# Leaky ReLU as one activation, and the second batch's k, numerators and kv in two parts each

## The chip, the core and the metric

The kernel runs on one core of a Trainium2 chip. The time is device time in microseconds (us) of one execution. Engines are named as in the profile: PE (TensorE matmul), PEld (its weight load), DVE (VectorE), ACT (ScalarE), POOL (GpSimd) and SP (SyncE, which here only issues DMAs).

## The reference

Three stages follow one another: linear attention with a feature map, a first MLP with leaky ReLU, and a second one of four experts. Cut to what is computed (batch 4, heads 8, sequence 576, head 64, 128 features):

```python
def phi(x):
    proj = einsum('bhsd,df->bhsf', x, w_phi)
    proj = proj - max(abs(proj), axis=-1, keepdims=True)
    return concatenate([exp(proj), exp(-proj)], axis=-1)
q_p, k_p = phi(q), phi(k)
kv  = einsum('bhsf,bhsd->bhfd', k_p, v)
z   = sum(k_p, axis=2)
num = einsum('bhsf,bhfd->bhsd', q_p, kv)
den = einsum('bhsf,bhf->bhs', q_p, z)[..., None] + 1e-06
x   = (num / den)                 # as 2304 tokens x 512
h   = x @ w_in                    # 512 x 2048
x   = maximum(0.01 * h, h) @ w_out    # 2048 x 512
# for each expert e of 4, p = domain_probs normalized:
out += p[:, e] * (maximum(x @ w1[e], 0) @ w2[e])
```

## The kernel before

Everything is in one program with four batches. For each batch the attention is done by head pairs (four per batch), and its output x stays on chip as xh and xl, one part of 128 rows for each head pair. The first MLP of a batch is done in 16 blocks of 128 hidden rows, in groups of four. The second MLP comes after the last batch's first MLP, from about 640 us, and the change doesn't touch it.

**Precision.** A matmul of plain f32 operands is recorded as two passes. In the other way an operand is written as a high part in fp32r and a low part (operand less high part, also fp32r), and three matmuls are made: high by high, high by low, low by high. The helper `hilo` (line 113) makes the parts: the high one as a copy on ACT (L117) or as a cast on DVE (L115; `VHI`, line 67, says which names go to DVE), the low one always as a subtraction on DVE (L118). `DIRECT` (line 37) says for each batch which operands stay plain f32: k (`k_prep`, L172, and the projection L204), n (the numerators with their e and kv: `kv_side` L250, `q_exp` L310, `q_num` L335) and q (the queries). Where kv is in two parts they are kvh and kvl (L258, L259); where k is, they are kh and kl; where e is, qh and ql.

**The attention's steps.** `load`, `load_v`, `load_q` bring kraw, v and qraw. `k_feat` makes in three parts the projection pk (PE L204), its absolute maximum m (DVE L209), the difference ky (DVE L216) and the exponentials kp and kt (ACT L227). `kv_side` accumulates kvp (PE L242). `q_prep` makes qr: a cast (DVE L273, or ACT L275) and its low part (DVE L276). `q_proj` makes pq (PE L292), copies it to pc (ACT) and reduces it over partitions to mb on POOL (L296). `q_sub` subtracts (DVE L301), `q_exp` makes e (ACT), and `q_num` the numerators nm (PE L335), which ACT copies to nf. `x_den` and `x_rec` bring the denominators ds by DMA into a small tile, make their reciprocals, write them to a scratch dr in DRAM (L362) and read them back spread over partitions as rb (L365). `x_mul` multiplies to xr (DVE L381) and splits it to xh (ACT) and xl (DVE L118).

**The first MLP.** `moe1_up` makes hp in PSUM (PE L506, 24 matmuls of 288 columns for each block), from it hs, 0.01 times it (ACT L518), and g, the larger of both (DVE L520), and splits g to gt. `moe1_down` (PE L538) accumulates op over four blocks. In batch 0 the weights come as 64-bit words: `w64_dma` (L445) loads 1 MB as r64, `w64_split` converts on ACT (L460) and DVE (L461, L464, L467) to w32, splits that to wt (L117, L118), and stores w32 to DRAM (L471), where the later batches load it.

**Order.** The steps of an attention have due times (`TIMES`), by which they are sorted; those of batch b+1 are spread over the first MLP of batch b (`LO`, `HI`). A scheduler with a simulated timeline then orders the instructions of each engine. Each engine works strictly in its order, and SP's one queue issues nearly all loads and stores. SBUF tiles of one row of 576 come from one pool of 19 buffers, whatever their name; PSUM tiles come from a pool of three buffers (hp, op, pq, the wide pk) and one of two (pk, kvp, nm).

Of the kernel before, what the change touches and what calls it, by code (L numbers as in the profile page):

```python
# [10 lines left out]
AF = mybir.ActivationFunctionType  # L11
ALU = mybir.AluOpType
# [21 lines left out]
WIDE = (1, 0, 0, 0)  # L34
INPL = (1, 0, 1, 0)

DIRECT = ('knq', 'kn', '', '')

TIMES = (
    (  # L40
# [39 lines left out]
def body(ctx, tc, kT, qT, vh, w_phi, w_in, w_out, probs, w1, w2, out):  # L80
    nc = tc.nc
# [22 lines left out]
    def unit(name, dt=F32):  # L104
        return up.tile([128, S], dt, tag="u", name=name)

    def two(name):
        return ps2.tile([128, 2, 512], F32, tag="two", name=name)
# [4 lines left out]
    def hilo(hi, lo, src, name, b):  # L113
        if name in VHI[min(b, 2)]:
            nc.vector.tensor_copy(hi, src)  # L115
        else:
            nc.scalar.copy(out=hi, in_=src)  # L117
        nc.vector.tensor_tensor(out=lo, in0=src, in1=hi.bitcast(F32), op=ALU.subtract)  # L118
# [52 lines left out]
    def k_prep(b, hp):  # L171
        kraw = raws[b, hp]  # L172
        if "k" in DIRECT[b]:
            kfs[b, hp] = kraw, None
# [56 lines left out]
    def kv_side(b, hp, h):  # L231
# [17 lines left out]
        if h == 1:  # L249
            if "n" in DIRECT[b]:  # L250
                kv = up.tile([128, 4, 128], F32, tag="u", name="kv")
# [14 lines left out]
    def q_prep(b, h):  # L266
        qraw = raws[b, "q", h]
        if "q" in DIRECT[b]:
            qrs[b, h] = qraw
# [11 lines left out]
    def q_proj(b, h):  # L281
        qr = qrs.pop((b, h))
        pq = two("pq")
        for n in range(2):
            o = pq[:, n, 0:HS]
            xs_ = qr[:, n * HS : (n + 1) * HS]
            if "q" in DIRECT[b]:

# [17 lines left out]
    def q_exp(b, h, n):  # L306
        mb = ys[b, h]
        e = unit("e")
        for j in range(2):
# [5 lines left out]
            )  # L315
        if "n" in DIRECT[b]:
            es[b, h, n] = e, None
# [100 lines left out]
    def attn(b, lo, hi):  # L418

        A = []  # L420
        for p in range(NP):
            T = TIMES[p if b == 0 else NP]
            for t, (f, h, a) in zip(T, STEPS):
                i = p if h is None else 2 * p + h
                A.append((p + t, lambda f=f, i=i, a=a: f(b, i, *a)))
        A.sort(key=lambda x: x[0])
        t0, t1 = A[0][0], A[-1][0]
        return [(lo + (hi - lo) * (t - t0) / (t1 - t0), f) for t, f in A]
# [68 lines left out]
    def moe1_up(F, n):  # L497
        x = xs[F // NF]
        wi = wt1[0, F]
        if n == 0:  # L500
            hps[F] = two("hp")
        hp = hps[F]
        for kk in range(KK):
            assert ("x", F // NF, kk) in made
            for i, (a, z) in enumerate(PASS):
                nc.tensor.matmul(  # L506
                    hp[:, n, 0:HS],
                    lhsT=wi[:, a, kk * 128 : (kk + 1) * 128],
                    rhs=x[z][:, kk, n * HS : (n + 1) * HS],
                    start=(kk == 0 and i == 0),  # L510
                    stop=(kk == KK - 1 and i == 2),
                )
        if n == 0:
            return
        hv = hp[:, :, 0:HS]
        hs = unit("hs")
        hs3 = hs.rearrange("p (a s) -> p a s", a=2)
        nc.scalar.mul(out=hs3, in_=hv, mul=0.01)  # L518
        g = unit("g")
        nc.vector.tensor_tensor(  # L520
            out=g.rearrange("p (a s) -> p a s", a=2), in0=hv, in1=hs3, op=ALU.max
        )
        gt = gp.tile([128, 2, S], F32R, tag="g", name="gt")
        hilo(gt[:, 0], gt[:, 1], g, 'g', F // NF + 1)
        gts[F] = gt
# [27 lines left out]
    def moe1_group(G):  # L553


        def up(F, n):
            if n == 0:
                w1_dma(0, F + 2)
                w1_split(0, F + 1)
                w1_dma(1, F)  # L560
            elif F:
                w1_split(1, F - 1)
            moe1_up(F, n)

        def down(d, n):
            if G == B * NF // GF and d == 0 and n == 0:
                w1_split(1, G * GF - 1)
            moe1_down(G - 1, d, n)

        M = []  # L570
        for kind, i in ORDER:
            if kind == "u" and G < B * NF // GF:
                M += [lambda i=i, n=n: up(G * GF + i, n) for n in range(2)]
            elif kind == "d" and G > 0:
                M += [lambda i=i, n=n: down(i, n) for n in range(2)]
        return M
# [96 lines left out]
    def w2_sums(r):  # L673
        pool, tag = (m2["r"], "r") if m2 else (wp, "w")
        s = pool.tile([128, 4, 256], F32, tag=tag, name="rs")
        for o, x, y, op in (
            (s[:, 0], r[:, 0], r[:, 1], ALU.add),
            (s[:, 1], s[:, 0], r[:, 2], ALU.subtract),
            (s[:, 2], r[:, 2], r[:, 0], ALU.subtract),
            (s[:, 3], r[:, 3], s[:, 1], ALU.subtract),  # L680
        ):
            kept(nc.gpsimd.tensor_tensor(out=o, in0=x, in1=y, op=op))  # L682
        return s
# [158 lines left out]
    def spread(fs, lo, hi):  # L842
        return [(lo + (hi - lo) * i / len(fs), f) for i, f in enumerate(fs)]
# [9 lines left out]
    for b in range(B):  # L853
# [3 lines left out]
        if b + 1 < B:  # L857
            a = attn(b + 1, b + LO[b], b + HI[b])
        else:
            early = x2_steps(0)  # L860
            a = spread(early[:4], b + 0.1, b + 0.9)
# [11 lines left out]
    s = w2_sums(r)  # L873
# [64 lines left out]
```

## Time and profile before

| what | us |
|---|---|
| three runs | 1379.39, 1382.25, 1383.28 |
| their median | 1382.25 |
| the profiled execution | 1380.63 |
| its span | 1378.8 |

The span of the profiled execution is 1.8 us shorter than its time. Over the span PE is busy 98%, PEld 92%, DVE 59%, ACT 48% and POOL 41%. These shares are averages over stages: up to about 110 us batch 0's attention is alone, or overlaps with the first blocks of its MLP; from there to about 610 us run the first MLPs of all batches with the attention of the next ones; then comes the second MLP. A wait is read from the timeline, where the idle time ahead of an instruction stands in brackets with what ended it. A busy PE may run at a low granted clock, or with gaps between short matmuls, so its spacing is read too.

### The profile page before, as it was taken

Reading aid. Unit: us, or ns where it says so; the run is one execution under the profiler, and the core shown is the slowest. Engines: PE = TensorE matmul, PEld = TensorE weight load, DVE = VectorE, ACT = ScalarE, POOL = GpSimd, SP = SyncE. Lnnn points to the kernel's source line nnn. Section 1 sums busy time; section 2 is a strip of 40 time slices with the busy share of each in tenths; the row PEclk is TensorE's granted clock in tenths of the full one; section 3 lists DMA queues with packets and bytes.
Section 4 is the critical chain, followed back from the end, with each engine's and each line's share of the span. In section 5 each row is a group of like instructions: output and inputs, shape, how many; then the busy total and the mean of one; then the engine's idle time right before and its main releaser. Section 6 shows DMA issues by size and latency. Waiting matters only on the chain.

```text
span 1378.8 us, 21301 instructions
## 1 busy us (share of the span) xinstructions
PE 1352.1 (98%) x8105; PEld 1262.2 (92%) x8105; DVE 817.8 (59%) x1285; ACT 657.9 (48%) x1201; POOL 567.8 (41%) x398
## 2 busy tenths in 40 slices
PE   8979999999999999999999999999999999999998
PEld 6778999999999999998999999999999999899997
DVE  4589999678786656553555445445454444554444
ACT  5657657676576435424343443434443343433331
POOL 3211102111111000027767666767767675565651
PEclk9989999999999999999999999999999999999999
DMA  6466645333332222302212122321121232122111
GB/s 220 113 217 234 220 167 166 111 120 105 109 103 66 75 86 73 104 24 94 75 61 77 62 68 71 107 77 62 62 77 62 77 107 77 62 64 76 61 62 62
DMA packets 78518, 134.94 MB, mean 98 GB/s; under 512 B 12240, under 2 KB 22608, under 8 KB 78416
## 3 DMA queue, kind: packets, MB, share of 16 engines
q1 hardware_dynamic: 78416, 133.58, 29.8%
q8 instruction: 64, 1.05, 0.3%
q14 instruction: 38, 0.31, 0.1%
HBM read 120.30 MB, written 13.18 MB: 97 GB/s over the span
## 4 chain that ended last, share of the span: by engine, by line
PE 95%; DVE 1%; DMA 1%; issue 1%; ACT 1%; POOL 1%; SPq 0%; POOLq 0%; ACTq 0%; DVEq 0%
PE po L761 29%; PE hp L506 15%; PE op L538 14%; PE py L722 11%; PE pv L722 7%; PE px L722 7%; PE kvp L242 5%; PE nm L335 4%; PE pk L204 2%; PE pq L292 1%; PE pq L289 1%; DMA qraw<-qT 1%; POOL wul L704 0%; DMA r<-w 0%; DMA ds<-nf 0%
## 5 line engine op out<-in xcount | busy, mean ns | idle before, releaser
L761 PE MATMUL po<-wd,gh 128*128 128x512 f32 x1152 | 387.7, 391 | 0.9 <-POOL wd L714 0.9
L777 DVE SCALAR_TENSOR_TENSOR ob<-po,pe,ob 128x512 f32<-128x512 f32 x270 | 201.6, 749 | 216.6 <-PE po L761 216.6
L761 PEld LDWEIGHTS po<-wd,gh 128*128 128x128 f32 x1152 | 216.6, 188 | 42.3 <-POOL wd L714 1.3
L761 PE MATMUL po<-wd,gl 128*128 128x512 f32 x576 | 226.2, 393 | 0.0
L538 PE MATMUL op<-gt,wt 128*128 128x288 f32 x1536 | 219.9, 297 | 1.5 <-DVE gt L118 0.8
L296 POOL PARTITION_ALL_REDUCE mb<-pc x32 | 72.3, 2266 | 355.7 <-ACT pc L294 294.7
L506 PE MATMUL hp<-xh,wt 128*128 128x288 f32 x1024 | 216.2, 298 | 0.0
L538 PEld LDWEIGHTS op<-gt,wt 128*128 128x128 f32 x1536 | 207.9, 188 | 2.9 <-DVE gt L118 1.0
L506 PEld LDWEIGHTS hp<-xh,wt 128*128 128x128 f32 x1024 | 167.5, 188 | 1.0 <-ACT wt L117 0.3
L506 PE MATMUL hp<-xl,wt 128*128 128x288 f32 x512 | 151.8, 297 | 0.0
L714 POOL TENSOR_TENSOR wd<-r,wd 128x1024 fp32r<-128x1024 f32 x48 | 114.9, 2394 | 89.4 <-ACT wd L710 89.4
L722 PE MATMUL py<-xo,wuh 128*128 128x384 f32 x576 | 148.3, 339 | 0.7 <-DVE pz L827 0.7
L682 POOL TENSOR_TENSOR rs<-r 128x256 f32<-128x256 f32 x96 | 71.1, 741 | 188.8 <-DMA r<-w 188.8
L704 POOL TENSOR_TENSOR wul<-rs,wuh 128x1024 fp32r<-128x1024 f32 x48 | 115.5, 2406 | 65.9 <-ACT wuh L699 65.9
L704 POOL TENSOR_TENSOR wul<-r,wuh 128x768 fp32r<-128x768 f32 x48 | 88.8, 1851 | 85.7 <-ACT wuh L699 85.7
L761 PEld LDWEIGHTS po<-wd,gl 128*128 128x128 f32 x576 | 108.2, 188 | 15.2
L722 PEld LDWEIGHTS py<-xo,wuh 128*128 128x128 f32 x576 | 104.9, 188 | 4.6 <-DVE pz L827 1.0
L722 PE MATMUL px<-xo,wuh 128*128 128x384 f32 x384 | 98.9, 338 | 0.7 <-DVE acc L551 0.7
L722 PE MATMUL pv<-xo,wuh 128*128 128x384 f32 x384 | 99.1, 339 | 0.0
L722 PE MATMUL py<-xo,wul 128*128 128x384 f32 x288 | 97.3, 338 | 0.0
L506 PEld LDWEIGHTS hp<-xl,wt 128*128 128x128 f32 x512 | 96.3, 188 | 0.4
L807 ACT COPY py<-px 128x384 f32<-128x384 f32 x48 | 22.2, 463 | 143.4 <-PE px L722 137.3
(114 smaller groups left out, 2349.9 us busy)
## 6 DMA issues: line engine op xcount, KB each, us to landing
r<-w SPq DMA_DIRECT2D x192, 256.0 KB, 2.8
wr<-w SPq DMA_DIRECT2D x96, 256.0 KB, 2.7
qraw<-qT SPq DMA_DIRECT2D x32, 288.0 KB, 3.7
r<-w_out SPq DMA_DIRECT2D x9, 1024.0 KB, 9.0
r<-w_in SPq DMA_DIRECT2D x8, 1024.0 KB, 6.2
w<-w SPq DMA_DIRECT2D x32, 256.0 KB, 2.8
v<-vh SPq DMA_DIRECT2D x16, 480.0 KB, 4.0
kraw<-kT SPq DMA_DIRECT2D x16, 288.0 KB, 4.0
```

Of the source, the lines that this page charges most:

```text
L204: nc.tensor.matmul(o, lhsT=x[:, cs], rhs=w, start=(i == 0), stop=(i == len(P) - 1))
L242: nc.tensor.matmul(kvp[:, a * 128 : (a + 1) * 128], lhsT=lhs, rhs=v[:, c, h * D : h * D + 128], start=(c == 0), stop=(c == 4),)
L296: nc.gpsimd.partition_all_reduce(mb, pc, 128, bass_isa.ReduceOp.absmax)
L335: nc.tensor.matmul(o, lhsT=a[:, 2 * (h % 2) + j], rhs=x[:, j * HS : (j + 1) * HS], start=(j == 0 and i == 0), stop=(j == 1 and i == len(P) ...
L506: nc.tensor.matmul(hp[:, n, 0:HS], lhsT=wi[:, a, kk * 128 : (kk + 1) * 128], rhs=x[z][:, kk, n * HS : (n + 1) * HS], start=(kk == 0 and i ...
L538: nc.tensor.matmul(op[:, n, 0:HS], lhsT=wt1[1, C * GF + f][:, a, d * 128 : (d + 1) * 128], rhs=gts[C * GF + f][:, z, n * HS : (n + 1) * HS ...
L682: kept(nc.gpsimd.tensor_tensor(out=o, in0=x, in1=y, op=op))
L704: kept(nc.gpsimd.tensor_tensor(out=lo[:, at], in0=(r[:, 1:4], s)[i], in1=hi[:, at].bitcast(F32), op=ALU.subtract))
L714: kept(nc.gpsimd.tensor_tensor(out=d[:, 1], in0=r2, in1=d[:, 0].bitcast(F32), op=ALU.subtract))
L722: kept(nc.tensor.matmul(out, lhsT=ws[w][:, AOPS[a], kk * 128 : (kk + 1) * 128], rhs=xo[z][:, kk], start=first and n == 0, stop=n == 5, ski ...
L761: kept(nc.tensor.matmul(op, lhsT=(gh, gl)[z][:, 2 * f + t, q : q + 128], rhs=d[:, w, f], start=n == 0, stop=n == 5,))
L777: kept(nc.vector.scalar_tensor_tensor(out=o, in0=op, scalar=ps, in1=o, op0=ALU.mult, op1=ALU.add))
```

## The change

`DIRECT` loses "k" and "n" for batch 1, so its k, e and kv are written in two parts, as those of batches 2 and 3 are, and its projections and numerators are three matmuls in the place of one in plain f32. The leaky ReLU of all 64 blocks is one activation with slope 0.01 from PSUM on ACT in the place of a multiplication on ACT and a maximum on DVE. The names hs and its buffer go. The scheduler orders anew; lines from 518 on stand 3 lower.

```diff
-DIRECT = ('knq', 'kn', '', '')
+DIRECT = ('knq', '', '', '')
...
         hv = hp[:, :, 0:HS]
-        hs = unit("hs")
-        hs3 = hs.rearrange("p (a s) -> p a s", a=2)
-        nc.scalar.mul(out=hs3, in_=hv, mul=0.01)
         g = unit("g")
-        nc.vector.tensor_tensor(
-            out=g.rearrange("p (a s) -> p a s", a=2), in0=hv, in1=hs3, op=ALU.max
+        nc.scalar.activation(
+            out=g.rearrange("p (a s) -> p a s", a=2), in_=hv, func=AF.Prelu, alpha=0.01
         )
         gt = gp.tile([128, 2, S], F32R, tag="g", name="gt")
         hilo(gt[:, 0], gt[:, 1], g, 'g', F // NF + 1)
```

The first place is SP's queue around the last head pair of batch 0. In the rows, dr and rb are the reciprocals on their way to DRAM and back, r64 the 1 MB weight loads, w32 the store of a converted weight. Before:

```order
L154 DMA kraw_591<-kT 128x576
L362 DMA dr_598<-ds_564 128x9
L445 DMA r64_619<-w_in 128x2x1024
L445 DMA r64_631<-w_out 128x2x1024
L365 DMA rb_600<-dr_598 64x576 x2
L471 DMA w32_0_2_680<-w32_675 128x512
L166 DMA qraw_654<-qT 128x576
```

The same queue after:

```order
L154 DMA kraw_599<-kT 128x576
L445 DMA r64_631<-w_in 128x2x1024
L445 DMA r64_643<-w_out 128x2x1024
L362 DMA dr_606<-ds_568 128x9
L471 DMA w32_0_2_696<-w32_691 128x512
L365 DMA rb_608<-dr_606 64x576 x2
L166 DMA qraw_668<-qT 128x576
```

The write to dr moved behind both weight loads, and the store of a weight ahead of rb.

The second place is DVE's queue up to the low part of the queries of batch 1, head 5 (qr, L276). Weight steps are L461, L464, L467 and wt. Its last rows before:

```order
L467 SCALAR_TENSOR_TENSOR w32_1006<-r64_786,w32_1006 128x512
L118 TENSOR_TENSOR wt_928<-w32_921,wt_928 128x512
L461 TENSOR_SCALAR w32_1150<-w32_1150 128x512
L273 CAST qr_956<-qraw_919 128x576
L359 TENSOR_SCALAR ds_1178<-ds_1178 128x9
L118 TENSOR_TENSOR wt_979<-w32_972,wt_979 128x512
L118 TENSOR_TENSOR gt_947<-g_945,gt_947 128x576
L464 SCALAR_TENSOR_TENSOR w32_1150<-r64_970,w32_1150 128x512
L276 TENSOR_TENSOR qr_956<-qraw_919,qr_956 64x576
```

And after:

```order
L209 TENSOR_REDUCE m_1146<-pk_1139 128x4
L464 SCALAR_TENSOR_TENSOR w32_1272<-r64_1048,w32_1272 128x512
L461 TENSOR_SCALAR w32_1461<-w32_1461 128x512
L464 SCALAR_TENSOR_TENSOR w32_1429<-r64_1036,w32_1429 128x512
L118 TENSOR_TENSOR ql_1019<-e_1015,qh_1018 128x576
L273 CAST qr_1022<-qraw_975 128x576
L467 SCALAR_TENSOR_TENSOR w32_1272<-r64_1048,w32_1272 128x512
L464 SCALAR_TENSOR_TENSOR w32_1461<-r64_1048,w32_1461 128x512
L118 TENSOR_TENSOR wt_1243<-w32_1236,wt_1243 128x512
L467 SCALAR_TENSOR_TENSOR w32_1429<-r64_1036,w32_1429 128x512
L276 TENSOR_TENSOR qr_1022<-qraw_975,qr_1022 64x576
```

From the end of the last xl of batch 0 to this instruction stand 47 instructions before and 63 after; a low part ql and steps of further weights stand ahead of it now.

The third place is PE's queue where the first matmuls of the MLP begin: kvp is the kv of batch 1's first head pair, kt the last part of its k features, pk a k projection, and hp is made from batch 0's xh. Before:

```order
L292 MATMUL pq_718<-qr_593,wl_92 128x288
L242 MATMUL kvp_707<-v_446,kp_571 128x128 x4
L204 MATMUL pk_765<-wraw_89,kraw_591 128x256 x2
L242 MATMUL kvp_707<-v_446,kt_572 128x128
L242 MATMUL kvp_707<-v_446,kp_571 128x128 x4
L242 MATMUL kvp_707<-v_446,kt_572 128x128
L242 MATMUL kvp_707<-v_446,kp_571 128x128 x4
L506 MATMUL hp_633<-xh_347,wt_478 128x288
L506 MATMUL hp_685<-xh_347,wt_628 128x288
```

And after:

```order
L292 MATMUL pq_742<-qr_601,wl_92 128x288
L242 MATMUL kvp_731<-v_446,kp_575 128x128 x4
L242 MATMUL kvp_731<-v_446,kt_576 128x128
L242 MATMUL kvp_731<-v_446,kp_575 128x128 x4
L242 MATMUL kvp_731<-v_446,kt_576 128x128
L242 MATMUL kvp_731<-v_446,kp_575 128x128 x4
L242 MATMUL kvp_731<-v_446,kt_576 128x128
L242 MATMUL kvp_731<-v_446,kp_575 128x128 x2
L506 MATMUL hp_645<-xh_347,wt_478 128x288
L506 MATMUL hp_701<-xh_347,wt_640 128x288
```

The k projection of the second head pair (pk) no longer stands between the kv matmuls.

## Rows read from the trace of the kernel before

**Rows 1.** The page: busy us, share of the span and instructions of each engine.
```profile
PE 1352.1 (98%) x8105; PEld 1262.2 (92%) x8105; DVE 817.8 (59%) x1285; ACT 657.9 (48%) x1201; POOL 567.8 (41%) x398
```

**Rows 2.** Windows by stage: us, busy of PE, PEld, DVE, ACT, POOL; clock; DMA; GB/s.
```profile
0.00:110.00 110.00, 91.80 (x504) 78.69 (x505) 70.41 (x116) 64.16 (x138) 26.40 (x16) 0.91 0.58 194
110.00:600.00 490.00, 489.02 (x3712) 485.06 (x3712) 367.82 (x578) 290.10 (x561) 46.10 (x20) 1.00 0.37 118
```

**Rows 3.** Timeline of PE, 36 to 44 us: start, length, engine, line, what.
```profile
37.20 1.89 PE L204 MATMUL pk<-wraw,kraw 128*128 128x256 f32 x8
38.92 4.04 PE L335 MATMUL nm<-e,kv 128*128 128x288 f32 x16
42.80 1.05 PE L242 MATMUL kvp<-v,kp 128*128 128x128 f32 x8
```

**Rows 4.** Chain of waits, pieces of 230 to 300 and 590 to 645: start, length, what.
```profile
233.67 0.71 PE pk L204 x6
...
591.00 3.19 PE hp L506 x24
```

**Rows 5.** Window of 86 to 118 us, columns as in rows 2.
```profile
86.00:118.00 32.00, 30.10 (x209) 28.16 (x207) 29.75 (x48) 24.16 (x51) 6.46 (x3) 0.97 0.70 255
```

**Rows 6.** Groups by line, whole span, then 86 to 118: busy, mean ns, idle.
```profile
L518 ACT ACTIVATE hs<-hp 128x576 f32<-128x576 f32 x64 | 41.6, 649 | 73.5 <-PE hp L506 72.8 <-DVE mb L301 0.7
L520 DVE TENSOR_TENSOR g<-hp,hs 128x576 f32<-128x576 f32 x64 | 48.2, 753 | 45.0 <-ACT hs L518 44.9
L118 DVE TENSOR_TENSOR ql<-e,qh 128x576 fp32r<-128x576 f32 x32 | 25.1, 784 | 4.1 <-ACT qh L117 4.0
...
L467 DVE SCALAR_TENSOR_TENSOR w<-r,w 128x512 uint32<-128x512 uint32 x7 | 4.5, 680 | 0.0
L520 DVE TENSOR_TENSOR g<-hp,hs 128x576 f32<-128x576 f32 x4 | 3.0, 749 | 1.2 <-ACT hs L518 1.2
L301 DVE TENSOR_TENSOR mb<-pc,mb 128x576 f32<-128x576 f32 x2 | 2.6, 1316 | 0.0
```

**Rows 7.** Timeline of DVE; in brackets the idle time ahead and what ended it.
```profile
65.03 1.53 DVE L381 TENSOR_TENSOR xr<-nf,rb 64x576 f32<-64x576 f32 x2 [4.53 <-DMA rb<-dr]
...
80.47 0.75 DVE L381 TENSOR_TENSOR xr<-nf,rb 64x576 f32<-64x576 f32 x1 [0.82 <-DMA rb<-dr]
...
85.19 0.75 DVE L118 TENSOR_TENSOR xl<-xr,xh 128x576 fp32r<-128x576 f32 x1
...
87.05 1.89 DVE L467 SCALAR_TENSOR_TENSOR w<-r,w 128x512 uint32<-128x512 uint32 x3
...
117.20 0.76 DVE L276 TENSOR_TENSOR qr<-qraw,qr 64x576 fp32r<-64x576 f32 x1
```

**Rows 8.** Chain of waits, the piece at 118 us.
```profile
118.34 0.53 PE pq L292 x4
```

**Rows 9.** Timeline of PE: three stops.
```profile
81.66 2.05 PE L204 MATMUL pk<-wraw,kraw 128*128 128x256 f32 x4 [5.35 <-issue]
...
609.99 1.85 PE L538 MATMUL op<-gt,wt 128*128 128x288 f32 x12 [0.71 <-DVE g L520]
...
612.60 9.04 PE L538 MATMUL op<-gt,wt 128*128 128x288 f32 x66 [0.76 <-DVE gt L118]
```

**Rows 10.** Timeline of SP's queue: when it issued these DMAs.
```profile
60.89 1.10 SPq L365 DMA_DIRECT2D rb<-dr  x2
...
70.99 0.43 SPq L445 DMA_DIRECT2D r<-w_in  x1
72.73 1.10 SPq L365 DMA_DIRECT2D rb<-dr  x2
...
79.68 0.34 SPq L471 DMA_DIRECT2D w<-w  x1
```

**Rows 11.** Windows of 8 us around two stops of PE, columns as in rows 2.
```profile
58.00:66.00 8.00, 5.96 (x21) 4.32 (x19) 3.37 (x8) 3.36 (x9) 0.00 (x0) 0.79 0.39 100
74.00:82.00 8.00, 2.59 (x11) 2.16 (x10) 4.01 (x8) 4.13 (x8) 0.00 (x0) 0.51 0.83 312
```

## The prediction

> **What bounds the kernel now.** I read the page first. PE is busy 98% of the span and every other engine 59% or less [rows 1]; so the question is where PE loses time. The windows by stage tell it: PE is busy 489.02 of 490.00 us from 110 to 600, idles 18.2 us before 110 [rows 2]. A busy PE is not PE at its peak, so I looked at the spacing too: 24 matmuls on 288 columns take 3.19 us in the chain, 0.133 us each [rows 4], and none comes faster anywhere. So from 110 us on a matmul saved is time saved and a wait added is time lost; nothing later gives it back. Before 110 us the waits decide. After 640 the change touches nothing.
>
> DVE is the engine to watch. From 86 to 118 us it is busy 29.75 of 32.00 us, beside PE's 30.10 [rows 5]. One pair of rows shows how near it is: DVE ends the low part of the queries of batch 1, head 5, at 117.20 + 0.76 = 117.96 [rows 7], and PE starts the projection that needs them at 118.34 [rows 8]. I call this the anchor.
>
> **PE's own work.** An f32 matmul runs as two passes. Sixteen passes of numerators, eight matmuls, start at 38.92 and the next work at 42.80: 0.485 us each; eight passes of the k projection start at 37.20 and the next work at 38.92: 0.43 a matmul [rows 3]. In two parts a numerator is three matmuls of 0.133 = 0.40, a k chunk three of 0.118 (six in 0.71 [rows 4]) = 0.355. Batch 1 has 32 numerator matmuls and 20 k chunks: 32 x 0.086 + 20 x 0.075 = **4.3 us less** for PE, nearly all of it behind 86 us, where PE is dense.
>
> **The leaky ReLU.** It takes away 64 DVE instructions of 753 ns and puts 64 activations in the place of 64 multiplies of 649 ns [rows 6]. Prelu itself isn't in the trace; the nearest row is that multiply, an activation of the same 128x576 shape out of PSUM, and I take its 649 ns. If Prelu took twice as long, ACT would have 4 x 0.65 = 2.6 us more between 86 and 118 us, where it has 7.8 us idle [rows 5]: still no bound. By the Trainium skill (ScalarE: Activation LUTs, "What ACT_TABLE_LOAD costs") an activation with immediate operands takes 186 ns + 0.833 ns a column whatever its function, 666 ns here as an estimate; the multiply's row agrees within 3%. What DVE saves is hidden while PE is dense. It shows in one place: at the end of the first MLP the chain of multiply, maximum, high part and low part lies open, and PE waits for it twice, until 609.99 and 612.60 [rows 9]. The maximum's 0.75 us falls out of that chain: **0.75 us less**.
>
> **What the two parts cost DVE.** Batch 1 gets 4 kh, 4 kl, 16 ql (784 ns [rows 6]) and 4 kvl on DVE and 16 qh on ACT, against 16 maxima that go in batch 0's MLP. More than the total it matters where they stand. DVE works strictly in its order, so I count what stands ahead of the anchor, from the end of xl, the low part of the last x of batch 0 (85.19 + 0.75 = 85.94 [rows 7]). An instruction moves the queue on by its duration less 0.08 us (three of 0.68 [rows 6] take 1.89 [rows 7]).
> Before: 10 of 576 columns at 0.67 (gt, g, mb), 21 of 512 at 0.60 (wt, w32, ky), 2 m at 0.61, 5 shifts at 0.34, 3 qr casts at 0.41, 3 qr low parts at 0.79, three small (the kinds without a row here by their means in the view of [rows 6]): 47 instructions, 26.7 us.
> After: 14 at 0.67 (6 ql, 4 gt, 2 kl, 2 mb), 26 at 0.60, 3 at 0.61, 8 at 0.34, 3 at 0.41, 2 kh at 0.38, 3 at 0.79, four small: 63 instructions, 34.9 us. The 8.2 us more are ql, kl, kh and kvl (6.7) and the weight conversions and reductions that the order moves ahead (4.2), less four maxima (2.7).
> Before took 32.0 us for its 26.7 (85.94 to 117.96): 1.9 us of waits, and 3.4 us in which instructions were stretched, as mb to a mean of 1316 ns [rows 6], beside POOL's three reductions [rows 5]. After has three there too, so I carry the 5.3 us over. It can be 3 (a late DVE waits for less) or 9 (each ql waits for a qh that ACT makes just before).
> Here a rule speaks against the change. By the Trainium skill (SBUF — State Buffer, "Who interferes with whom") a DVE instruction with two SBUF inputs contends with GpSimd's reads, one with at most one doesn't. The maximum read PSUM and SBUF, and its mean there is 749 ns, not stretched [rows 6], as the rule has it; ql and kl read SBUF twice. By the rule one instruction is caught per reduction, and 5.3 us stay; were the loss in proportion to the queue, it would be 5.3 x 34.9 / 26.7 = 6.9, and the sum 1.6 us worse.
>
> **Up to xl.** Here SP's order decides. Before, the rb load of the last head pair was issued at 72.73, shared the DMA engines with two 1 MB loads [rows 10], and DVE got it at 80.47, 7.7 us later [rows 7]. In after it stands behind the store of a converted weight, which waits for DVE's three steps on the w_in load. But that load no longer waits for dr and starts about 3 us earlier than its 70.99; so the store, at 79.68 before, goes at some 76.7 and rb at 77.1. An rb load without such company took 4.1 us, issued at 60.89 [rows 10] and used at 65.03 [rows 7]: xr at 81.2, or 84.8 with 7.7. I take the first, since the big loads are over by then. From xr to the end of xl DVE needs 5.5 us in both orders: 86.8 against 85.94, **0.9 us later**.
> PE loses a stop of 5.35 us before 81.66 [rows 9], whose releaser the row doesn't name; by the order it is the PSUM buffer that the last ky empties, and that stands behind xr on DVE. The stop isn't won: kvp needs kt, which comes from the last ky too. PE restarts at about 82.9, with less queued, and reaches the xl matmuls at about 89 in both.
>
> **The sum.** Anchor: 86.8 + 34.9 + 5.3 = 127.0 on DVE, PE at 127.1 instead of 118.34: 8.8 us later. PE then has less left: the 4.3 saved, less 1.6 used up by then (12 k chunks, 8 numerator matmuls), plus 13 down matmuls (1.7) that the new order does earlier: 4.4. That leaves +4.4. Such a stop costs clock too: from 58 to 66 PE was busy 5.96 of 8 us and the granted clock was 0.79, which is 0.21 x 8 = 1.7 us; from 74 to 82, busy 2.59 us, it was 0.51 [rows 11]. I take **1.7**. With the end's 0.75: 4.4 + 1.7 - 0.75 = **+5.3 us**. The profiled execution's 1380.63 becomes 1385.9; by the median of the runs, 1382.25, **1387.5**.
>
> **Rivals.**
> (a) *DVE absorbs it: no change.* For it: before, DVE waited because it was early, and a late one waits for nothing. With only the 34.9 us and no clock lost the anchor is at 121.7, and 121.8 - 118.34 - 4.4 - 0.75 = -1.7 us; with the 3.4 of stretching, +1.7: 1380.5 to 1384. Against it: six qh that are made just in time.
> (b) *Only PE's saving counts: faster.* DVE does the first k parts in its idle time before xl and the projection of head 5 finds its queries ready: -4.3 - 0.75 = -5, 1377. It decides if DVE is some 9 us further at xl than I have it. Against it: the order, in which 63 instructions stand between.
> (c) *rb is late: slower still.* With 7.7 us for rb behind the store, xl and the anchor come 3.6 us later and the clock stays low as long again (1.7): +10.6, 1393. Nothing between rb's issue and xl takes it up.
> (d) The activation could ignore its slope; it would cost the same, and no time hangs on it.
>
> **How the numbers follow.** A measurement of this kernel can tell about 0.3% (4.1 us) from no change. Forecast 0.43, (a) 0.32, (c) 0.11, (b) 0.14. The forecast lies 1 us over the bound of 1386.4, so 0.06 of its 0.43 goes to the middle: slower 0.48, within 0.38, faster 0.14. The range leaves out (b) and the far half of (c): 1380 to 1394.
>
> **What would show it.** Right: in after a PE wait of 5 us or more for DVE qr L276 between 115 and 130 us, DVE without a gap ahead of it, and a low clock behind it; xl at 86 to 88; then a dense PE to 600 with numerators at 0.133 a matmul; the wait before 612 shorter by 0.75. Wrong: no such wait (a, b); rb used after 83 (c); or an activation of hp well above 0.65 us.

## The result, and the profile after

| | before | after |
|---|---|---|
| median of five runs, us | 1379.52 | 1388.70 |
| lowest and highest, us | 1377.96 to 1383.28 | 1385.69 to 1389.69 |
| profiled execution, us | 1380.63 | 1385.69 |
| its span, us | 1378.8 | 1383.6 |

The changed kernel is slower: the ratio of the runs is 1.0058, with a 95% interval of 1.0046 to 1.0069, which is 8.0 us on 1379.5 (the two medians lie 9.2 apart). The forecast was 1387.5 and "slower", with 1380 to 1394 as its range. Of the two profiled executions one is 1.1 us above its kernel's median and the other 3.0 below, so the traces show 4.8 us (the spans) of the 8.0. The 3 us between stay unexplained by them. One execution of a later run, e10, took 2235.71 us at a granted clock of 0.557 and is left out of its ratio.

The page of the changed kernel, engines over the whole span, answers to [rows 1]; PE's share fell by a point:

```profile
PE 1348.5 (97%) x8157; PEld 1264.0 (91%) x8157; DVE 797.6 (58%) x1249; ACT 664.2 (48%) x1217; POOL 569.2 (41%) x398
```

The windows of 86 to 130 us, columns as in [rows 2], tell where: of before first,

```profile
86.00:130.00 44.00, 42.10 (x290) 39.48 (x288) 41.72 (x69) 31.97 (x66) 9.62 (x4) 0.98 0.69 248
```

and of after:

```profile
86.00:130.00 44.00, 33.40 (x235) 32.50 (x234) 38.59 (x64) 32.14 (x64) 10.52 (x4) 0.88 0.61 208
```

PE idles 10.6 us there, before it idled 1.9. Elsewhere the idle times hardly differ. The timeline of PE of the changed kernel (in brackets the idle time ahead, and what ended it) has these stops:

```profile
95.94 0.37 PE L292 MATMUL pq<-qr,wh 128*128 128x288 f32 x1 [2.06 <-DVE qr L276]
...
104.01 0.40 PE L335 MATMUL nm<-qh,kvh 128*128 128x288 f32 x1 [1.71 <-ACT nf L342]
...
106.15 0.61 PE L335 MATMUL nm<-qh,kvh 128*128 128x288 f32 x1 [0.73 <-ACT nf L342]
...
126.75 0.58 PE L292 MATMUL pq<-qr,wh 128*128 128x288 f32 x1 [6.11 <-DVE qr L276]
...
127.84 3.87 PE L535 MATMUL op<-gt,wt 128*128 128x288 f32 x22
131.55 0.29 PE L335 MATMUL nm<-qh,kvh 128*128 128x288 f32 x1
```

The stop of 6.11 us is the one that was forecast, at the projection of batch 1, head 5, with DVE's qr as releaser. The two rows after it show the clock: 22 down matmuls take 131.55 - 127.84 = 3.71 us, where 22 x 0.133 = 2.93 are usual, and the four of pq took 1.09 for 0.53. That is 1.3 us lost behind the stop; the granted clock from 86 to 130 is 0.88. The stop at 95.94 was not forecast; at 104 and 106 there are two for nf, before there was one of 1.66.

DVE in the changed kernel, its last xl of batch 0, and what it did until the low part of those queries:

```profile
82.80 0.75 DVE L118 TENSOR_TENSOR xl<-xr,xh 128x576 fp32r<-128x576 f32 x1
...
90.17 0.76 DVE L118 TENSOR_TENSOR gt<-g,gt 128x576 fp32r<-128x576 f32 x1 [3.48 <-ACT gt L117]
...
92.18 0.76 DVE L118 TENSOR_TENSOR ql<-e,qh 128x576 fp32r<-128x576 f32 x1 [0.58 <-ACT qh L117]
92.86 1.55 DVE L273 CAST qr<-qraw 128x576 fp32r<-128x576 f32 x1
...
121.96 0.47 DVE L273 CAST qr<-qraw 128x576 fp32r<-128x576 f32 x1
...
124.87 1.74 DVE L276 TENSOR_TENSOR qr<-qraw,qr 64x576 fp32r<-64x576 f32 x1
```

From 83.55 to 126.61 DVE needs 43.1 us for the 34.9 us of work counted in the prediction, so 8.2 us are waits and stretched instructions; before it was 5.3 [rows 7]. The longest wait, 3.48 us, is for the first gt, which ACT could make only when PE had the first block of the MLP done, as ACT's timeline shows:

```profile
88.26 0.65 ACT L517 ACTIVATE g<-hp 128x576 f32<-128x576 f32 x1 [3.46 <-PE hp L506]
```

PE's own work came out as worked out. Three numerator matmuls of the changed kernel start 0.13 us apart:

```profile
99.73 0.29 PE L335 MATMUL nm<-qh,kvh 128*128 128x288 f32 x1
99.87 0.29 PE L335 MATMUL nm<-ql,kvh 128*128 128x288 f32 x1
100.00 0.30 PE L335 MATMUL nm<-qh,kvl 128*128 128x288 f32 x1
```

And the new activation, in the groups by line, costs what the multiply did [rows 6]:

```profile
L517 ACT ACTIVATE g<-hp 128x576 f32<-128x576 f32 x64 | 41.4, 651 | 87.6 <-PE hp L506 84.8 <-DVE xr L381 1.7 <-DVE qr L276 0.5
```

So the account of the two profiled executions is: 8.7 us more of idle PE between 86 and 130, 0.6 less ahead of that, 0.2 more later, 1.3 of clock behind the stop, and 4.3 us less of work: +5.3 against the +4.8 of the spans. The half microsecond between lies in PE's busy time, which holds work and clock together: it fell by 3.6 us over the span (1352.1 to 1348.5), where these terms make 3.0.

### The profile page after: what moved, and what is told of

Same layout as the page of the kernel before. It is cut to its first block, busy times and chain, and to the rows that moved or that the text cites. A ratio compares the mean times of both kernels' runs of the same rounds, so it can differ in the third digit from the quotient of the medians.

```text
span 1383.6 us, 21389 instructions
## 1 busy us (share of the span) xinstructions
PE 1348.5 (97%) x8157; PEld 1264.0 (91%) x8157; DVE 797.6 (58%) x1249; ACT 664.2 (48%) x1217; POOL 569.2 (41%) x398
## 4 chain that ended last, share of the span: by engine, by line
PE 91%; DVE 4%; DMA 2%; issue 1%; ACT 1%; SPq 0%; POOL 0%; DVEq 0%; ACTq 0%; POOLq 0%
PE po L758 29%; PE op L535 14%; PE hp L506 13%; PE py L719 11%; PE pv L719 7%; PE px L719 7%; PE kvp L242 4%; PE nm L335 3%; PE pk L204 2%; PE pq L292 1%; DMA rb<-dr 1%; DMA r<-w_out 1%; DVE w L464 1%; DMA qraw<-qT 0%; DVE w L467 0%
## 5 line engine op out<-in xcount | busy, mean ns | idle before, releaser
L118 DVE TENSOR_TENSOR wt<-wr,wt 128x512 fp32r<-128x512 f32 x96 | 65.0, 695 | 70.3 <-ACT wt L117 67.6
```

## The experiments

The theory: DVE's queue ahead of the queries of head 5 makes the loss, by its length. The rivals: the activation itself; parts that are made just in time; no room on DVE at all; and, after the first runs, the numerators of particular head pairs. Each kernel is scheduled anew, so an edit changes more than one place, and the table is read with that in mind. Differences are the ratio less one, times 1379 us.

| run | what is in it | ratio and interval | us against before | PE busy of 86 to 130 | of 130 to 260 |
|---|---|---|---|---|---|
| before | | 1 | 0 | 42.10 | 129.02 |
| after | activation, all parts | 1.0058 (1.0046 to 1.0069) | +8.0 | 33.40 | 128.90 |
| e1 | activation alone | 1.0003 (0.9994 to 1.0012) | +0.4 | 41.00 | 130.00 |
| e2 | parts alone | 1.0133 (1.0118 to 1.0149) | +18.3 | 33.27 | 123.47 |
| e3 | after, high parts of k and q on ACT | 1.0037 (1.0024 to 1.0049) | +5.1 | 39.02 | 125.73 |
| e4 | after, queries on ACT and POOL | 1.0226 (1.0212 to 1.024) | +31.2 | 28.55 | 120.96 |
| e5 | activation, k in parts | 0.9989 (0.9981 to 0.9998) | -1.5 | 41.43 | 130.00 |
| e6 | activation, numerators in parts | 1.0048 (1.0036 to 1.006) | +6.6 | 39.55 | 125.72 |
| e7 | activation, both, pairs 2 and 3 | 0.9997 (0.9989 to 1.0006) | -0.4 | 40.40 | 129.44 |
| e8 | after, less weight conversion | 1.0029 (1.0018 to 1.004) | +4.0 | 34.35 | 130.00 |
| e9 | e5 and numerators of pairs 2 and 3 | 1.0001 (0.9991 to 1.0011) | +0.1 | 41.26 | 128.84 |
| e10 | e5 and numerators of pair 0 | 1.0011 (1.0001 to 1.002) | +1.5 | 38.34 | 130.00 |
| e11 | e5 and numerators of pair 1 | 1.0038 (1.0024 to 1.0051) | +5.2 | 36.81 | 129.30 |
| e12 | after, queries due earlier | 1.0037 (1.0024 to 1.005) | +5.1 | 37.71 | 127.88 |

### Which part does it: e1 and e2

e1 takes the changed kernel and gives batch 1 its plain f32 back:

```diff
-DIRECT = ('knq', '', '', '')
+DIRECT = ('knq', 'kn', '', '')
```

> The leaky ReLU as one activation alone; the second batch's k, numerators and kv stay in plain f32 as before. Theory (DVE's queue ahead of the projection of batch 1, head 5, makes the loss): four maxima less stand in that queue and no low parts come in, so PE finds those queries ready, and the time is within 2 us of before, rather below it (0 to -2 us). Rival (the activation itself, longer on ACT or late for the matmuls that follow it, makes the loss): +4 to +8 us.

e2 is the kernel before with the other edit:

```diff
-DIRECT = ('knq', 'kn', '', '')
+DIRECT = ('knq', '', '', '')
```

> The two parts alone; multiply and maximum stay as before. Theory (DVE's queue): 67 DVE instructions, 37.7 us of them, stand between the last xl and the queries of head 5, 2.8 us more than in the changed kernel, where PE waited 6.1 us for them. So a stop of about 9 us there, and 3 us more than the changed kernel: +11 us against before. Rival (the parts cost what they cost in matmuls and just-made operands, and DVE's load doesn't matter): as the changed kernel, +8 us, with a stop no longer than its 6.1.

e1 came out as the theory has it: the activation alone changes nothing that can be measured, though DVE loses 64 instructions of 0.75 us. e2 went the right way and too far, +18.3 for +11. At the place of the one stop of 6.11 us it has two, and more come later. The timeline of PE in e2 at that place, and then its windows:

```profile
122.69 3.63 PE L538 MATMUL op<-gt,wt 128*128 128x288 f32 x14 [3.26 <-DVE gt L118]
...
128.68 0.37 PE L292 MATMUL pq<-qr,wh 128*128 128x288 f32 x1 [2.36 <-ACT kvh L258]
```

```profile
86.00:130.00 44.00, 33.27 (x225) 31.79 (x225) 39.93 (x67) 30.90 (x62) 6.65 (x3) 0.92 0.51 182
130.00:260.00 130.00, 123.47 (x906) 121.17 (x905) 117.53 (x193) 82.07 (x161) 16.54 (x7) 0.96 0.52 173
```

From 130 to 260 PE idles 6.5 us, which neither before nor after does. So the maxima that the activation removes are worth nothing where DVE has room (e1) and 10 us beside the parts (e2 against after): the two edits of the change are not independent. What does it is more than one instruction; whether it is the time that the maxima take on DVE or the link that each adds between hs and g, e2 doesn't tell apart.

### Off that queue: e3 and e4

e3 moves high parts to ACT:

```diff
-VHI = ({"g", "w"}, {"k", "q"}, {"k"})
+VHI = ({"g", "w"}, set(), {"k"})
```

> The changed kernel with the high parts of batch 1's k and queries made on ACT in the place of DVE. Theory (DVE's queue): 49 instructions, 27.7 us, stand ahead of those queries, 7.2 less than in the changed kernel, so the stop of 6.1 us goes, and with it about 1 us of clock: 7 us less than the changed kernel, about +1 against before. Rival (the loss is in qh and kl made just in time and in the denser PE before 110): ACT has seven more high parts to make, so it gets no better, +8 to +10.

The stop of 6.11 us did go: the timeline of PE in e3 shows no stop between 106 and 180. The gain was 3 us, not 7, which lies between the theory's and the rival's number. Against the changed kernel PE idles 5.6 us less from 86 to 130 (the stops at 95, 103 and 105 are still there) and 3.2 us more from 130 to 260. Two of the stops that came there, in the timeline of PE:

```profile
191.99 0.40 PE L335 MATMUL nm<-qh,kvh 128*128 128x288 f32 x1 [1.18 <-ACT qh L117]
...
235.43 2.13 PE L535 MATMUL op<-gt,wt 128*128 128x288 f32 x14 [0.92 <-DVE wt L118]
```

e4 takes batch 1's queries off DVE, with the high parts on ACT and the low ones on POOL:

```diff
-VHI = ({"g", "w"}, {"k", "q"}, {"k"})
+VHI = ({"g", "w"}, {"k"}, {"k"})
...
-        nc.vector.tensor_tensor(
+        (nc.gpsimd if b == 1 else nc.vector).tensor_tensor(
             out=qr[D:128], in0=qraw[D:128], in1=qr[D:128].bitcast(F32), op=ALU.subtract
```

> The changed kernel with batch 1's queries taken off DVE: high part on ACT, low part on POOL. Theory (DVE's queue): PE no longer waits for DVE there; if POOL is in time, 7 us less than the changed kernel, 0 to +1 against before; kv's low part behind it on DVE is the next to look at. Rival (just-made qh and kl): +8. Rival (POOL's reads of two SBUF operands stretch DVE's low parts): DVE's ql and kl above 0.85 us in the mean between 86 and 130, and half of the gain lost, +4.

Neither theory had this: +31 us. The timelines of PE and of POOL in e4 show it. PE stops for 15.93 us:

```profile
87.95 0.61 PE L292 MATMUL pq<-qr,wh 128*128 128x288 f32 x1 [15.93 <-POOL qr L276]
```

```profile
75.03 4.30 POOL L296 PARTITION_ALL_REDUCE mb<-pc  x2 [7.33 <-issue]
86.50 1.39 POOL L276 TENSOR_TENSOR qr<-qraw,qr 64x576 fp32r<-64x576 f32 x1 [7.17 <-DVE wt L118]
```

POOL works in its order too. The low part stood behind two reductions and then waited 7.17 us more, by the row for a DVE instruction. It costs POOL 1.39 us where DVE takes 0.76. The run says that POOL is no place for queries that PE is about to need; of the rest it tells nothing.

### How much of it is the queue's length: e8

```diff
-        nc.vector.scalar_tensor_tensor(
-            out=wu, in0=lo, scalar=29, in1=wu, op0=ALU.logical_shift_right, op1=ALU.bitwise_or
-        )
```

> The changed kernel without the third step of the weight conversion (L467), so the lowest bits of the first MLP's weights are left out; DVE loses 32 x 0.6 = 19 us of work in batch 0's MLP, 5 us of it ahead of the projection of head 5. Both theories: the stops for DVE go. One stop: 30.0 us in the queue, the stop shrinks by 4.9 to about 1: -4 to -5 against the changed kernel, +3 against before. No room on DVE anywhere: 19 us more than repay the 6.6 added, so PE's 4.3 us come through: -3 to -5 us against before.

Measured: +4.0, 4.0 less than the changed kernel. The number is close to what one stop was to give, but not for its reason: the stop was to shrink to about 1 us, and it is still there. The timeline of PE in e8:

```profile
124.05 0.58 PE L292 MATMUL pq<-qr,wh 128*128 128x288 f32 x1 [5.02 <-DVE qr L276]
```

And of DVE ahead of it:

```profile
81.94 0.75 DVE L118 TENSOR_TENSOR xl<-xr,xh 128x576 fp32r<-128x576 f32 x1
...
89.36 0.76 DVE L118 TENSOR_TENSOR gt<-g,gt 128x576 fp32r<-128x576 f32 x1 [4.91 <-ACT gt L117]
...
117.06 0.69 DVE L209 TENSOR_REDUCE m<-pk 128x4 f32<-128x512 f32 x1 [1.29 <-PE pk L204]
...
122.16 1.74 DVE L276 TENSOR_TENSOR qr<-qraw,qr 64x576 fp32r<-64x576 f32 x1
```

From the end of xl, 82.69, to 123.90 pass 41.2 us for 30.0 us of work: 4.9 us less of work made the stretch only 1.9 us shorter, since the waits and stretched instructions in it grew from 8.2 to 11.2. DVE idles there for gt (4.91 us for 3.48), which hangs on PE's first block, and at 117.06 for PE's pk (1.29 us). So the work counted from xl is not what sets the queries' time; and against "no room on DVE" the run speaks more clearly still: 19 us less of DVE's work did not bring PE's 4.3 us out.

### Which parts: e5, e6 and e7

e5 and e6 take half of the change for batch 1:

```diff
-DIRECT = ('knq', '', '', '')
+DIRECT = ('knq', 'n', '', '')
```

> The changed kernel with the second batch's numerators and kv back in plain f32: only k is in two parts, with the activation. DVE gets 4 kh and 4 kl (4.2 us) and loses 16 maxima (10.7 us) in batch 0's MLP. Theory (DVE's queue ahead of the projection of head 5): 44 instructions, 23.8 us, stand there, less than before's 26.7, so no stop; PE saves 20 x 0.075 = 1.5 us: -1 to -2 us against before. Rival (k in two parts is itself what hurts, kl made just in time in the dense stretch of 86 to 110): a stop for kl or m there, +2 to +4 us.

```diff
-DIRECT = ('knq', '', '', '')
+DIRECT = ('knq', 'k', '', '')
```

> The changed kernel with the second batch's k back in plain f32: only numerators and kv are in two parts, with the activation. DVE gets 16 ql and 4 kvl (13.1 us) and loses 16 maxima (10.7 us). Theory of one stop (DVE's queue ahead of head 5): 52 instructions, 29.6 us, stand there and PE has about the same to do, so the stop of 6.1 us shrinks to 0 to 1; PE saves 32 x 0.086 = 2.8 us: -1 to -3 us against before. Rival, formed from the run with the high parts on ACT, where that stop went and others came between 180 and 240 us: DVE has no room anywhere from 86 to 240 us, and what is added to it in the sum, here 2.4 us, ends as stops of PE somewhere: 0 to +1 us, with stops between 180 and 240.

e5 gave -1.5 us, as worked out from PE's work: k in two parts with the activation is better than the kernel before by a tenth of a per cent (the interval ends at 0.9998), and than the changed one by 0.7. e6 gave +6.6, which neither of its expectations had (-1 to -3, and 0 to +1), so the loss is with the numerators. The stop for the queries of head 5 is not in e6, as the count of its queue had it; but one came at 193, for which the chain of waits of e6 tells the cause:

```profile
185.75 0.26 PE nm L335 x2
186.01 3.97 PE hp L506 x30
189.98 0.55 PE nm L335 x4
...
190.55 0.40 ACT nf L342
190.95 0.68 ACT e L310 x2
```

The timelines of ACT and of DVE show what waits, and when kvl was made:

```profile
190.55 0.40 ACT L342 COPY nf<-nm 128x288 f32<-128x288 f32 x1 [4.97 <-PE nm L335]
```

```profile
185.11 0.69 DVE L259 TENSOR_TENSOR kvl<-kvp,kvh 128x512 fp32r<-128x512 f32 x1
```

The timeline of PE shows the effect:

```profile
193.27 0.40 PE L335 MATMUL nm<-qh,kvh 128*128 128x288 f32 x1 [1.83 <-ACT qh L117]
194.38 1.06 PE L535 MATMUL op<-gt,wt 128*128 128x288 f32 x6 [0.71 <-ACT g L517]
```

In plain f32 a numerator is made when kv and e are there. In parts it also waits for kvl. PE's order here begins a numerator with the two matmuls that need kvh, does 30 MLP matmuls, and then comes back for the one with kvl. ACT's copy to nf stands in ACT's order for all that time (4.97 us idle), and e, qh and g stand behind it; when it is released, PE has used up what it could do. DVE had kvl done at 185.80, as those 30 matmuls began, so it is PE's order and not kvl that holds up the copy. It is an in-order wait on a third engine that neither a count of DVE's work nor a share of busy time shows. Such a wait need not cost anything: from 130 to 260 ACT waits 15.6 us in all for numerators in the changed kernel, 11.6 in e5, and PE idles 1.1 and 0.0 us there. So e6's stop at 193 is not what makes the changed kernel slow.

e7 keeps all parts for head pairs 2 and 3 alone:

```diff
+HP1 = 2
+
+
+def plain(x, b, hp):
+    return x in ("kn" if b == 1 and hp < HP1 else DIRECT[b])
...
-        if "k" in DIRECT[b]:
+        if plain("k", b, hp):
...
-            if "n" in DIRECT[b]:
+            if plain("n", b, hp):
...
-        if "n" in DIRECT[b]:
+        if plain("n", b, h // 2):
```

> The changed kernel, but of the second batch only head pairs 2 and 3 are in two parts; 0 and 1 stay in plain f32. DVE gets 8.6 us and loses 10.7 in batch 0's MLP; PE saves 2.1 us. Theory of one stop: 24.5 us of DVE stand ahead of the projection of head 5, no stop, -2 us against before. Rival (no room on DVE from 86 to 240): the sum is 2 us below before's, so no stops either: -2 us. Both fall if it is slower than before.

Measured: -0.4, no stop of over 0.5 us between 106 and 260, and no loss; the 2 us of gain that both theories had are not seen.

### Which head pairs: e9, e10 and e11

All three are e5 with the numerators of some head pairs in parts, by the same function:

```diff
+    return x in DIRECT[b] or (b == 1 and x == "n" and hp < 2)
```

> The changed kernel, with the second batch's k in two parts throughout, its numerators and kv in two parts for head pairs 2 and 3 only, and in plain f32 for 0 and 1. Theory (the numerators of head pairs 0 and 1 do the harm, by their place among the first MLP blocks and the weight conversions; k's parts and the later numerators find room): PE saves 1.5 + 1.4 = 2.9 us and no new stop comes: -3 us against before. Rival (any numerators in two parts bring a stop of PE, a few us, somewhere between 180 and 240): 0 to +3 us.

```diff
+    return x in DIRECT[b] or (b == 1 and x == "n" and hp > 0)
```

> As the last, but the numerators and kv in two parts for head pair 0 only. Ahead of the queries of head 5 stand 47 DVE instructions of 26.3 us. Theory (the place in DVE's order of those queries decides, and only the numerators of head pair 1 move it): no stop of PE for them, and 1.5 + 0.7 us less work: -2 us against before. Rival (the numerators' extra links, qh to ql and kvh to kvl, cost where the MLP begins, 86 to 110): +1 to +3 us.

```diff
+    return x in DIRECT[b] or (b == 1 and x == "n" and hp != 1)
```

> As the last, but head pair 1 only. Ahead of the queries of head 5 stand 61 instructions of 33.5 us, and PE has 38.2 us of matmuls to do till there: 2.3 us less of a stop than the changed kernel's 6.1. Theory (their place in DVE's order): a stop of about 4 us between 115 and 130 with its clock, less 2.2 us of saved work: +2 to +3 us against before, and the worse of the two head pairs by 4 to 5 us. Rival (both cost the same): within 1 us of the run with head pair 0.

Against e5 the numerators of pair 1 cost 6.7 us, those of pair 0 cost 3.0, those of pairs 2 and 3 together 1.6, each to within some 2 us. The worst is the pair that was named, though +5.2 against before is more than the +2 to +3 expected; its stop was put at about 4 us, and the timeline of PE in e11 has

```profile
124.67 0.58 PE L339 MATMUL nm<-qh,kvh 128*128 128x288 f32 x1 [4.64 <-DVE ky L220]
```

with another releaser, ky, which stands next to those queries in DVE's order. e10 has no such stop, as expected, and still gains nothing: its +1.5 is the rival's number. Its stops lie where the MLP begins; the first of them, in the timeline of PE, is the one of the changed kernel at 95.94, which neither before nor e5 has:

```profile
94.73 0.37 PE L296 MATMUL pq<-qr,wh 128*128 128x288 f32 x1 [2.06 <-DVE qr L280]
```

Its releaser is again DVE's part of some queries, those of batch 1, head 3, and not a copy between the numerators' parts. DVE's timeline in e10 shows them behind two ql, beside a reduction of POOL that begins at 91.57; the second ql and the cast:

```profile
90.97 0.76 DVE L122 TENSOR_TENSOR ql<-e,qh 128x576 fp32r<-128x576 f32 x1 [0.58 <-ACT qh L121]
91.64 1.55 DVE L277 CAST qr<-qraw 128x576 fp32r<-128x576 f32 x1
```

In e5, where batch 1 has no ql, the cast comes ahead of the first gt, where DVE would idle:

```profile
86.74 0.45 DVE L273 CAST qr<-qraw 128x576 fp32r<-128x576 f32 x1
```

The changed kernel, e6 and e8 have this cast late and at 1.55 us, e9 and e11 early and at 0.45 or 0.46. So for pair 0 too the place of queries in DVE's order shows, only of other queries than those of head 5.

e9 disappointed: 0.1 where -3 was expected. Its profiled execution, 1376.30, has no stop of over 0.5 us from 104 to 260, but it is the fastest of its twelve runs, which go up to 1381.87. What the slower ones do stays open.

### The order alone: e12

```diff
             for t, (f, h, a) in zip(T, STEPS):
+                if b == 1 and f in (load_q, q_prep):
+                    t -= 0.4
```

> The changed kernel with all its work, but batch 1's loads of queries and their splitting due 0.4 of a head pair's time earlier, which puts them well ahead in DVE's order. Theory (the place in DVE's order of the queries of head 5, not the amount of work): no stop for them, 6 to 7 us less than the changed kernel, 0 to +2 against before. Rival (the added links of the numerators bring a stop elsewhere, as between 180 and 200 us in the run with numerators alone): +5 to +8 against before.

All work is kept, and the queries are made early. Their stop is gone, and 2.9 of the 8.0 us come back: +5.1, which is the rival's number and not the theory's. The timeline of PE in e12 shows waits for low parts and copies in its place, the first for the numerators' kvl:

```profile
108.50 0.40 PE L335 MATMUL nm<-qh,kvl 128*128 128x288 f32 x1 [2.93 <-DVE kvl L259]
...
115.93 0.40 PE L537 MATMUL op<-gt,wt 128*128 128x288 f32 x1 [1.70 <-ACT gt L117]
```

Two quite different edits, e3 and e12, take the stop away, and both are left with +5.1 us: each nets 3 of the 8 us, not the 6 to 7 that were expected. But each also brings idle time of PE with it. For e3 it stands above. e12 has 4.3 us less than the changed kernel from 86 to 130, 1.0 more from 130 to 260, and 3.2 more before 86, as the windows show, of the changed kernel first and then of e12:

```profile
0.00:86.00 86.00, 70.31 (x382) 59.70 (x383) 55.84 (x92) 48.19 (x101) 21.95 (x14) 0.92 0.56 181
```

```profile
0.00:86.00 86.00, 67.16 (x355) 56.46 (x356) 56.57 (x89) 46.91 (x99) 22.55 (x14) 0.95 0.59 195
```

Whether that time is the price of the edit or the old loss in a new place is not shown. So what the stop alone is worth stays open; its removal gave 3 us here, twice.

## Why the prediction was right, and where its steps were off

**PE's saving** (4.3 us) held by the spacing, 0.13 a matmul. In the runs it shows less clearly: e5's -1.5 us (interval -2.6 to -0.3) fits the 1.5 of k, but e7 and e9, with 2.1 and 2.9 us of it, gave -0.4 and +0.1.

**The activation** held: 651 ns against the 649 taken, and e1 shows that it is hidden. By the Trainium skill (ScalarE: Activation LUTs, "What ACT_TABLE_LOAD costs") it is 666 ns as an estimate; the row is 2% below.

**The end's 0.75 us** failed. Before, PE waited 0.71 and 0.76 us there [rows 9]; after, once, 1.48. The maximum fell out of the chain, and the low part behind it took its time. The timelines of POOL and DVE, before,

```profile
609.52 2.41 POOL L704 TENSOR_TENSOR wul<-rs,wuh 128x1024 fp32r<-128x1024 f32 x1
```

```profile
610.67 1.87 DVE L118 TENSOR_TENSOR gt<-g,gt 128x576 fp32r<-128x576 f32 x1 [0.74 <-ACT gt L117]
```

and after:

```profile
614.34 2.37 POOL L701 TENSOR_TENSOR wul<-rs,wuh 128x1024 fp32r<-128x1024 f32 x1
```

```profile
614.74 2.59 DVE L118 TENSOR_TENSOR gt<-g,gt 128x576 fp32r<-128x576 f32 x1 [3.79 <-ACT gt L117]
```

The low part begins beside a POOL instruction and ends 0.61 us after it before (612.54 and 611.93), 0.62 after it after (617.33 and 616.71), whenever it began. Two shorter cases agree: a gt ended at 606.76 beside a POOL instruction that ended at 606.14 before, and one at 610.96 beside one that ended at 610.34 after, 0.62 us each. By the Trainium skill (SBUF — State Buffer, "Who interferes with whom") a DVE instruction with two SBUF inputs contends with a GpSimd instruction that reads SBUF, over a shared port pair that the section calls "an exclusive lock"; both pairs of rows agree. The prediction used that rule for the queue and not here, where it decided.

**Up to xl** was mis-sized: xl ends at 83.55, not 86.8 (and 81.2 + 5.5 makes 86.7). The loads behind the store came as forecast, only sooner: rb was issued at 74.86 instead of 77.1, and used 3.0 us later, as SP's and DVE's timelines show:

```profile
74.86 1.35 SPq L365 DMA_DIRECT2D rb<-dr  x2
```

```profile
77.89 0.75 DVE L381 TENSOR_TENSOR xr<-nf,rb 64x576 f32<-64x576 f32 x1 [0.68 <-DMA rb<-dr]
```

**The queue's waits** were mis-sized the other way: 8.2 us where 5.3 were carried over. The stretching was about as before, 2.9 us of the 8.2 for 3.4; the waits themselves rose from 1.9 to 5.3, most of it the 3.48 for gt. The two errors, 3.3 us early and 2.9 us more of waits, cancelled, and the queries came at 126.61 on DVE for 127.0. That they cancelled so closely was luck, though not luck alone: e8 shows that what DVE saves there it mostly waits away. The step that failed is "I count what stands ahead of the anchor, from the end of xl": PE's first block sets when the first gt can begin, and DVE idles for it, 3.48 us here and 4.91 in e8. Behind it the count isn't safe either: from the first gt to the queries, e8 is 1.9 us shorter (36.4 to 34.5) for 52 instructions in the place of 58, some 3.6 us of work.

**The stretched instructions** were forecast as one for each reduction of POOL. The cast of 1.55 us at 92.86 is one; such a cast takes 0.47 at 121.96. The 1.74 us of the queries' own low part at 124.87 is another. The cast reads one SBUF tile only, which the prediction's form of the rule leaves out; the same section of the Trainium skill says that casts too can contend, when their operands meet the conditions of a mode that uses both ports. This row agrees that it contends, but the cast ended at 94.41 and POOL's reduction at 95.15, so it didn't wait for the whole of it. The stretching makes the queries 1.1 us later for which PE stops 2.06 us at 95.94. Beside the 6.11, the stops from 86 to 130 sum to 4.5 us, for 1.9 before. The prediction's sum has no such term and needs none as long as head 5's queries set the time: had PE not stopped earlier, it would have waited longer for them. The term matters once that stop is taken away, as in e3, where 5.0 us of stops are left there.

**The clock** was put at 1.7 us; behind the stop it was 1.3.

**The sum** was +5.3 on the profiled execution, and the spans differ by 4.8. By the runs it is 8.0. That the forecast of 1387.5 lies only 1.2 us from the measured median is in part luck: it stands on a median of 1382.25 before, which two more executions took to 1379.52. The direction, the place and the releaser of the stop were right; that this one stop is the whole cause is not shown. The theory as stated in the experiments, that its removal gives 6 to 7 us back, fell with e3 and e12. What the runs support is narrower: the numerators of head pairs 0 and 1 in two parts cost some 3 and 7 us, and the stop at 126.75 is the largest single place in which that shows. How they cost it is seen in part: their low parts move the queries back in DVE's order (the stops of 6.11 and 2.06 us), and added links (qh to ql, kvh to kvl, and ACT's copies between them) hold up in-order queues in e6 and e12. How the 8 us divide among these is argued and not shown, since a new schedule comes with each edit.

**Rivals.** (a), DVE absorbing it, did not come for this change; no change was measured in e1, e7 and e9, where DVE's work falls or what is added comes late. (b), faster, came true only for e5. (c) did not come: rb was early.

## What to carry to other kernels

A stop that an edit brings in is a place, not yet a price: before counting its length as the gain of its removal, take it away in two ways and see what the end does, and where the idle time goes. Work split into high and low parts can cost more by what it pushes back in in-order queues than in engine time, so look at what the new parts now stand ahead of (here the queries), and split first where the operands are ready long before (here k, and the late head pairs). A saving in a chain is worth nothing if the chain's last instruction ends with another engine's.

## What the runs showed of the hardware that was not expected

A DVE subtraction of two SBUF tiles that begins beside a POOL subtraction ends about 0.6 us after it, whether it began 1.15 or 0.40 us behind it: 1.87 and 2.59 us for what takes 0.75 alone. A DVE cast from SBUF that begins 0.07 or 0.08 us behind a partition reduction took 1.55 us for 0.47, in the changed kernel and alike in e6, e8 and e10, and ended before the reduction did (94.41 and 95.15 in the changed kernel). The low part of one head's queries, 64x576, took 1.39 us on POOL where DVE takes 0.76.
